# First scores as 16 packed 32x32 tiles, an ordered table of steps, v in strips of 32 partitions

## The chip, the cores and the metric

One core of a Trainium2 chip runs the whole program in one launch. The metric is the device time of one execution in microseconds (us), the median of several. The core's engines work side by side, each through its own list of instructions strictly in order: TensorE (PE; its weight loads, PEld, overlap its matmuls), VectorE (DVE), ScalarE (ACT), GpSimd (POOL), and SyncE (SP), which here issues the loads and stores. They wait for each other through semaphores.

## What is computed

```python
def attn(qq, kk, vv):                       # softmax attention, scale 1/8
    s = scale * qq @ kk.T;  a = exp(s - s.max(-1)); return (a / a.sum(-1)) @ vv
pp  = attn(p, k, v)                         # 8 batches x 8 heads: 32 packed rows over 576 tokens of 64
x   = attn(q, pp, pp)                       # 576 tokens over the 32 packed rows
logits = x @ phi                            # soft MoE: 8 experts x 4 slots, softmax over all 4608 tokens
slot_out = relu((softmax0(logits).T @ x) @ w1) @ w2
y   = softmax1(logits) @ slot_out
out = (mish(y @ w_in)) @ w_out              # 512 -> 2048 -> 512
```

All is float32; w_in and w_out lie as 64-bit words in memory and are converted on the chip.

## The kernel before

It goes through three phases: attention with the gathering of the slots, batch by batch; eight experts; the MLP. Only the attention's code and the order of the first loads are changed.

A **batch** (b) has its 8 heads in two groups of four (hq, and h4 within it). For each group, q and k arrive as one tile of 128 partitions (4 heads x 32 rows of 18 tokens). `tr_kq` transposes such a tile on VectorE in blocks of 32x32 (two transposes of 512 columns and one of 128). For k the destination of the large ones is interleaved by 4 elements; for q it is runs of 32. In v's tile partition 4r+a holds tokens that match this.

**First scores** (`s1`, p against k): p of four heads lies block-diagonally in a 128x128 weight, `pBD`, written by `bd_p`; k's transposed tile streams through, 4 matmuls of 288 columns for a group. `s1_act` takes the maximum over 576 columns on VectorE (`nmx`) and the exponential with its sum on ScalarE. `e1t` transposes the exponentials on TensorE (n = 0, 1: the groups; n = 2: the rest of 64 tokens) and ScalarE copies them out. `pv` multiplies them by v, `pv_c` scales, `pv_bd` transposes the packed rows and `pv_dg` writes them into a block-diagonal weight `ppBD` with four copies of 32 partitions.

**Second scores** (`s2`, q against the packed rows) come in two parts, z = 0 and 1: matmuls, `s2_mx` (maximum and difference, VectorE), `s2_exp` (ScalarE), `s2_norm` (sum and reciprocal, VectorE), `s2_mul` (GpSimd). `at` transposes them, `gmat` is the packed rows times phi, `lt` the logits. The steps `r_*` gather the slots with a running maximum: `r_mx`, `r_mr`, `r_row`, `r_d`, `r_de`, `r_dt`, `r_u`, `r_sel`, `r_si`.

What sets the order: the calls stand one after the other as written, and each engine's list follows from them. In the loop over b, second scores of batch b, `e1t` and `pv` of b+1, first scores of b+2 and the gathering of b-1 are interleaved. After the loop the last two batches run out, mixed with the conversion of the first eight w_in tiles (`cv_z`, `cv_u`, `cv_m`) and with idle matmuls as fillers (`warm1`). PSUM tiles of all small products share three buffers (`ps_t`), so each waits for the one three before it to be read out.

**Loads** are a list of jobs on SyncE's queue: for each batch k of b+2, v of b+1, q of b+1; then eight w_in tiles, then w1 and w2 of the experts with the rest of w_in between, then w_out. `pump` issues the next job when its buffer in a ring is free; a job waits there for everything ahead of it. `vr` (the last two tokens of each row of v) has two buffers, so vr of batch b waits for `pv` of batch b-2. The experts' tiles need the rings' places, and the first of them come free when expert 0 has run its first product (`hp`).

Of the kernel before, what the change touches and what calls it, by code (L numbers as in the profile page):

```python
# [9 lines left out]
F32 = mybir.dt.float32  # L10
# [9 lines left out]
def kernel(  # L20
# [22 lines left out]
    NB = 5  # L43
# [132 lines left out]
    for nm, b in (("k", 0), ("v", 0), ("q", 0), ("k", 1)):  # L176
        add_qkv(nm, b)
# [40 lines left out]
    e1_0 = win[2][:, 2 * HQ * D:2 * HQ * D + S]  # L218
    pT = win[0][:, 0:2 * B * HQ * J].rearrange("p (a c j) -> p a c j", c=2, j=J)
# [3 lines left out]
    def load_phi():  # L223
# [17 lines left out]
    pBD, ppBD = (  # L241
        [w.rearrange("p (b q c j) -> p b q c j", b=2, q=HQ, c=2)[:, i] for i in range(2)] for w in (win[1], win[3])
    )
    for t in pBD + ppBD:
        nc.gpsimd.memset(t, 0.0)
    warm = ps_s1.tile([128, 2, 512], F32, name="s1", tag="s1")
    for i in range(5):
        nc.tensor.matmul(warm[:, 0, 0:256], lhsT=ident, rhs=pBD[1][:, 0].rearrange("p c j -> p (c j)"), start=True, stop=True)
    load_phi()
    ids = const.tile([128, 32], F32, name="ids")  # L250
    idrep = const.tile([128, 128], F32, name="idrep")

    def consts2():
        nc.vector.reduce_sum(out=ids, in_=ident.rearrange("p (g m) -> p m g", g=4), axis=AX.X)
        nc.vector.tensor_copy(out=idrep.rearrange("p (g m) -> p g m", g=4), in_=ids[:, None, :].to_broadcast([128, 4, 32]))
# [22 lines left out]

    def cv_u(nm, i, name, dst, z, tv, fold):
# [17 lines left out]
    bgq = []  # L297

    def bg(n):

        for _ in range(n):
            if bgq:
                bgq.pop(0)()

    def bg_early():
        ts = [[] for _ in EARLY]
        z = [lambda t=t, x=x: t.extend(cv_z(*x)) for t, x in zip(ts, EARLY)]
        bgq.extend(z[0:2])
        for j, t in enumerate(ts):
            bgq.extend(lambda f=f, t=t: f(*t) for f in (cv_u, cv_m))  # L310
            bgq.extend(z[j + 2:j + 3])

# [9 lines left out]
    def tr_kq(nm, b, hq):  # L322
# [3 lines left out]
        main, rem = (slice(0, 512), slice(512, 576)) if nm == "k" else (slice(64, 576), slice(0, 64))  # L326
        st[b][nm + "T", hq] = T
        for dh in range(2):
            nc.vector.transpose(  # L329
                out=T[:, dh, main].rearrange(  # L330
                    "p (i r a) -> p a i r" if nm == "k" else "p (i a r) -> p a i r", i=4, a=4,
                ),
                in_=x[:, 0:16 * D].rearrange("p (a i dh dl) -> p dh a i dl", a=4, i=4, dh=2)[:, dh],
            )
        nc.vector.transpose(
            out=T[:, :, rem].rearrange("p dh (i r) -> p i dh r", i=2),
            in_=x[:, 16 * D:18 * D].rearrange("p (i dh dl) -> p i dh dl", i=2, dh=2),
        )
# [10 lines left out]
    def bd_p(b):  # L349
        if b < 2:  # L350
            return diag(pBD[b % 2], pT[:, b * HQ:(b + 1) * HQ], scale)
        for h4 in range(4):
            r = slice(32 * h4, 32 * h4 + 32)
            nc.gpsimd.tensor_scalar_mul(out=pBD[b % 2][r, :, :, r], in0=pT[r, b * HQ:(b + 1) * HQ], scalar1=scale)

    def s1(b, hq):
        d = st[b]
        kT = d.pop(("kT", hq))
        if hq == 0:
            d["sm"] = t1.tile([128, HQ], F32, name="sm1", tag="sm1")  # L360
        if (b, hq) == (0, 1):
            ps = ps_s2.tile([128, 2, 512], F32, name="s1", tag="s2_1")
        else:
# [1156 lines left out]
```

## Time and profile before

| what | value |
|---|---|
| median of 3 runs (lowest, highest) | 658.74 us (657.58, 659.43) |
| profiled execution | 660.98 us, of which the span 659.2 us |
| TensorE, VectorE, ScalarE, GpSimd busy in the span | 619.2 (94%), 502.6 (76%), 338.9 (51%), 57.3 us (9%) |
| chain that ended last, by engine | PE 73%, DVE 14%, DMA 5%, ACT 4% |
| moved by the queues | 89.61 MB, nearly all in the first 250 us |

The shares mix three phases with different limits, so they say little of the attention, which ends at about 164 us. Stretches are read one by one: in each, the engine whose busy time comes nearest to the stretch's length leads, and the share of the DMA queues says whether loads could go faster.

### The profile page before, as it was taken

Reading aid. Unit: us, or ns where it says so; the run is one execution under the profiler, and the core shown is the slowest. Engines: PE = TensorE matmul, PEld = TensorE weight load, DVE = VectorE, ACT = ScalarE, POOL = GpSimd, SP = SyncE. Lnnn points to the kernel's source line nnn. Section 1 sums busy time; section 2 is a strip of 40 time slices with the busy share of each in tenths; the row PEclk is TensorE's granted clock in tenths of the full one; section 3 lists DMA queues with packets and bytes.
Section 4 is the critical chain, followed back from the end, with each engine's and each line's share of the span. In section 5 each row is a group of like instructions: output and inputs, shape, how many; then the busy total and the mean of one; then the engine's idle time right before and its main releaser. Section 6 shows DMA issues by size and latency. Waiting matters only on the chain.

```text
span 659.2 us, 14426 instructions
## 1 busy us (share of the span) xinstructions
PE 619.2 (94%) x5878; PEld 533.4 (81%) x5878; DVE 502.6 (76%) x997; ACT 338.9 (51%) x681; POOL 57.3 (9%) x78
## 2 busy tenths in 40 slices
PE   7899999998969969999999999999999999999996
PEld 5677777776315538888888999999999999999996
DVE  5998888796571188988688987887788778877883
ACT  3344555645431367655364655555555555555551
POOL 5122222121040040000000000000000000000000
PEclk9899999997979989999999999999999999999998
DMA  8998946997799981011101100110011001100111
GB/s 285 325 295 315 310 156 239 402 397 290 243 397 403 393 354 33 0 33 33 32 1 33 33 16 18 33 33 17 18 33 33 21 14 33 33 25 9 33 33 33
DMA packets 42354, 89.61 MB, mean 136 GB/s; under 512 B 10928, under 2 KB 19248, under 8 KB 42288
## 3 DMA queue, kind: packets, MB, share of 16 engines
q1 hardware_dynamic: 41840, 88.36, 38.5%
q8 instruction: 46, 0.75, 0.5%
q10 hardware_dynamic: 192, 0.26, 0.2%
q14 instruction: 20, 0.16, 0.1%
q0 software_dynamic: 256, 0.07, 0.0%
HBM read 79.23 MB, written 9.44 MB: 135 GB/s over the span
## 4 chain that ended last, share of the span: by engine, by line
PE 73%; DVE 14%; DMA 5%; ACT 4%; issue 1%; SPq 1%; POOL 0%; DVEq 0%; ACTq 0%; POOLq 0%
PE o L1316 42%; PE so L1316 14%; PE h L1201 5%; DVE kT L329 4%; DMA r_w<-in_moe_w_dram 3%; PE hp L981 2%; PE so L1008 2%; DVE A L501 1%; DMA r_p<-in_p_dram 1%; DVE mx L500 1%; PE cp L1060 1%; PE s L481 1%; DVE nmx L377 1%; PE s L814 1%; ACT AT L539 1%
## 5 line engine op out<-in xcount | busy, mean ns | idle before, releaser
L1316 PE MATMUL o<-whi,gh 128*128 128x256 f32 (+1 forms) x444 | 117.5, 309 | 3.3 <-DVE osb L1357 2.2
L1316 PE MATMUL o<-wlo,gh 128*128 128x256 f32 (+1 forms) x444 | 116.5, 307 | 0.0
L1232 ACT CAST gh<-s 128x512 fp32r<-128x512 f32 x116 | 53.8, 511 | 109.4 <-PE o L1316 109.4
L1206 ACT ACTIVATE s<-h 128x512 f32<-128x512 f32 x144 | 83.7, 594 | 49.8 <-PE h L1201 49.7
L1316 PE MATMUL o<-whi,gl 128*128 128x256 f32 (+1 forms) x444 | 95.5, 305 | 0.0
L1316 PEld LDWEIGHTS o<-whi,gh 128*128 128x128 f32 x444 | 83.4, 190 | 8.1 <-ACT Sh L1233 2.4
L1316 PEld LDWEIGHTS o<-wlo,gh 128*128 128x128 f32 x444 | 84.2, 190 | 4.7
L1235 DVE TENSOR_TENSOR gl<-s,gh 128x512 fp32r<-128x512 f32 x116 | 59.5, 554 | 34.9 <-ACT gh L1232 34.9
L1236 DVE TENSOR_TENSOR Sl<-S,Sh 128x1024 fp32r<-128x1024 f32 x58 | 70.9, 1223 | 10.4 <-ACT Sh L1233 8.9
L1316 PEld LDWEIGHTS o<-whi,gl 128*128 128x128 f32 x444 | 71.5, 188 | 4.5
L1316 PE MATMUL o<-T,Sh 128*128 128x256 f32 x464 | 73.8, 281 | 0.0
L1316 PEld LDWEIGHTS o<-T,Sh 128*128 128x128 f32 x464 | 63.1, 188 | 0.0
L1233 ACT CAST Sh<-S 128x1024 fp32r<-128x1024 f32 x58 | 60.9, 1050 | 3.4 <-DVE S L1217 2.1
L1217 DVE TENSOR_TENSOR S<-s 128x256 f32<-128x256 f32 x116 | 48.8, 421 | 14.9 <-ACT s L1206 14.9
L1201 PE MATMUL h<-CS,MS 128*128 128x256 f32 x288 | 55.8, 284 | 0.0
L1316 PE MATMUL o<-T,Sl 128*128 128x256 f32 x232 | 46.9, 284 | 0.0
L1201 PEld LDWEIGHTS h<-CS,MS 128*128 128x128 f32 x288 | 44.0, 188 | 2.2 <-issue 1.0
L1357 DVE TENSOR_TENSOR osb<-osb,o 128x256 f32<-128x256 f32 x86 | 32.7, 417 | 8.2 <-PE o L1316 5.0
L1316 PE MATMUL so<-T,Sh 128*128 128x256 f32 (+1 forms) x232 | 38.6, 289 | 0.0
L367 PE MATMUL s<-kT,win 128*128 128x288 f32 x128 | 34.8, 415 | 2.8 <-ACT win L379 2.5
L1316 PEld LDWEIGHTS o<-T,Sl 128*128 128x128 f32 x232 | 35.9, 190 | 0.0
L481 PE MATMUL s<-win,qT 128*128 128x128 f32 x256 | 33.5, 286 | 1.8 <-ACT win L347 1.8
(254 smaller groups left out, 1132.1 us busy)
## 6 DMA issues: line engine op xcount, KB each, us to landing
r_w<-in_moe_w_dram SPq DMA_DIRECT2D x63, 512.0 KB, 10.5
r_k<-in_k_dram SPq DMA_DIRECT2D x16, 576.0 KB, 7.4
r_q<-in_q_dram SPq DMA_DIRECT2D x16, 576.0 KB, 4.8
r_v<-in_v_dram SPq DMA_DIRECT2D x64, 128.0 KB, 5.5
r_wi<-in_moe_w_in_dram SPq DMA_DIRECT2D x16, 512.0 KB, 9.1
r_wo<-in_moe_w_out_dram SPq DMA_DIRECT2D x16, 512.0 KB, 8.8
out_dram<-osb SPq DMA_DIRECT2D x64, 128.0 KB, 2.2
vr<-in_v_dram SPq DMA_DIRECT2D x16, 64.0 KB, 2.6
```

The costliest lines, as they stand in the source:

```text
L329: nc.vector.transpose(out=T[:, dh, main].rearrange("p (i r a) -> p a i r" if nm == "k" else "p (i a r) -> p a i r", i=4, a=4,), in_=x[:, 0 ...
L367: nc.tensor.matmul(ps[:, n, 0:288], lhsT=pBD[b % 2][:, hq, dh], rhs=kT[:, dh, 288 * n:288 * n + 288], start=(dh == 0), stop=(dh == 1),)
L481: nc.tensor.matmul(ps[:, k - lo], lhsT=d["qT", hq][:, dh, 64 + 128 * i:192 + 128 * i], rhs=ppBD[b % 2][:, hq, dh], start=(dh == 0), stop=( ...
L1201: nc.tensor.matmul(hp[:, 256 * f:256 * f + 256], lhsT=MS[:, 128 * ft:128 * ft + 128], rhs=CS[:, 256 * n:256 * n + 256], start=True, stop=True,
L1206: nc.scalar.activation(out=s, in_=hp.rearrange("p (f n) -> p f n", f=2), func=AF.Mish)
L1217: nc.vector.tensor_tensor(out=S[:, k], in0=x, in1=y, op=op)
L1232: nc.scalar.copy(out=gh[:, f, t], in_=s[:, f, t])
L1233: nc.scalar.copy(out=Sh, in_=S)
L1235: nc.vector.tensor_tensor(out=gl[:, f, t], in0=s[:, f, t], in1=gh[:, f, t].bitcast(F32), op=ALU.subtract)
L1236: nc.vector.tensor_tensor(out=Sl, in0=S, in1=Sh.bitcast(F32), op=ALU.subtract)
L1316: nc.tensor.matmul(o, lhsT=lhsT, rhs=rhs, start=first, stop=stop)
L1357: add = lambda o, x, y: nc.vector.tensor_tensor(out=o, in0=x, in1=y, op=ALU.add)
```

## The change

- **First scores in tiles.** `s1` does both groups of a batch at once: 32 matmuls of 32 rows by 32 columns, each row strip one head of four (h4), each column strip one of four combinations of group and half of the tokens (th). The weight is p transposed as it is, scaled in place; `pBD` and `bd_p` are gone. The results of the four h4 go to four PSUM banks, in the buffers of tags s1 and s2_1. Each head's tokens now lie in two halves on different partitions, so the maxima of the two halves meet through a matmul with a swapped negative identity (`s1_sw`) and a minimum (`s1_nm`); four exponentials of 288 columns follow; the sums meet through a selection matrix (`s1_sum`, 8 matmuls).
- **Transposes.** The k tile's transposes write runs of 32; those of q's 16x64 part are one instruction instead of two. `e1t` n = 2 becomes 8 ordinary matmuls of 32 columns against the identity, copied out in two pieces.
- **v.** A group of v comes in four DMAs, each to 32 partitions, 4 heads at once (runs of 1 KB as before), in the order of strips 0, 2, 1, 3. Before, it was one DMA per head to 128 partitions.
- **Queue.** k of batch 1 stands ahead of v and q of batch 0.
- **Order.** A table of named steps (`STEPS`) and three texts: HEAD, LOOP (50 steps and more, once each for b = 2, 3, 4) and TAIL. Copies out of PSUM are steps of their own (`e0c`, `a0c`, `dc`). In names, k0, k1, q0, q1 are transposes of the two groups, m, x, n, l with a or b the maximum, exponential, sum and product of the second scores' two parts, a0 to a2 `at`, bd and dg `pv_bd` and `pv_dg`. The last batch's second scores come in two parts instead of three; the buffers of transposed q and k are given to the weights after the last second scores; fillers drop from 21 matmuls to 6.

```diff
     def job_v(b, hq):
         def emit(t):
-            for h4 in range(4):
+            for a in (0, 2, 1, 3):
                 nc.sync.dma_start(
-                    out=t[:, 4 * h4 * D:4 * h4 * D + 4 * D],
-                    in_=v[b, 4 * hq + h4].rearrange("(r j) d -> r (j d)", j=18)[:, 0:16 * D].rearrange(
-                        "r (a x) -> r a x", a=4,
-                    ),
+                    out=t[32 * a:32 * a + 32, 0:16 * D].rearrange("r (h x) -> r h x", h=4),
+                    in_=v[b, 4 * hq:4 * hq + 4].rearrange("h (r j) d -> r h (j d)", j=18)[:, :, 4 * D * a:4 * D * a + 4 * D],
                 )
...
-    for nm, b in (("k", 0), ("v", 0), ("q", 0), ("k", 1)):
+    for nm, b in (("k", 0), ("k", 1), ("v", 0), ("q", 0)):
...
+        if nm == "k":
+            for th in range(2):
+                nc.vector.transpose(
+                    out=T[:, :, 288 * th:288 * th + 256].rearrange("p dh (i a r) -> p a i dh r", i=2, a=4),
+                    in_=x[:, 0:16 * D].rearrange("p (a t i dh dl) -> p t a i dh dl", a=4, t=2, i=2, dh=2)[:, th],
+                )
...
+    def s1(b):
...
+        for dh in range(2):
+            for hq in range(HQ):
+                for th in range(2):
+                    c = 64 * hq + 32 * th
+                    for h4 in range(4):
+                        r = slice(32 * h4, 32 * h4 + 32)
+                        nc.tensor.matmul(
+                            ps[h4 // 2][c:c + 32, h4 % 2, 0:288], lhsT=pT[r, b * HQ + hq, dh],
+                            rhs=kT[hq][r, dh, 288 * th:288 * th + 288], start=(dh == 0), stop=(dh == 1),
+                        )
...
+        for i, ps in enumerate(st[b]["s1"]):
+            nc.vector.reduce_max(out=mx[:, 2 * i:2 * i + 2], in_=ps[:, :, 0:288], axis=AX.X)
...
+        nc.tensor.matmul(sw, lhsT=minus_sw, rhs=st[b]["mx1"], start=True, stop=True)
...
+        nc.vector.scalar_tensor_tensor(out=nm, in0=d.pop("mx1"), scalar=-1.0, in1=d.pop("sw"), op0=ALU.mult, op1=ALU.min)
...
+        for i in range(4):
+            nc.scalar.activation(
+                out=d["e1"][i], in_=ps[i // 2][:, i % 2, 0:288], func=AF.Exp,
+                bias=nm[:, i:i + 1], scale=1.0, accum_out=d["sm"][:, i:i + 1],
+            )
...
+                nc.tensor.matmul(
+                    rp[32 * h4:32 * h4 + 32, hq:hq + 1], lhsT=sel[:, hq], rhs=d["sm"][:, h4:h4 + 1], start=True, stop=True,
+                )
...
         for h4 in range(4):
...
+            for th in range(2):
                 nc.tensor.matmul(
...
+                    tp[32 * th:32 * th + 32, h4], lhsT=d["e1"][h4][:, 256:288], rhs=ident, start=True, stop=True,
                 )
...
+    LOOP = """
+        s2a rmx mr k1 e0 e1 row e0c d s2b e1c dc ma k0 de dt xa mb e2 dtc na e2c xb us nb sum sumc s1 usc da la pv sel
+        mx1 pvc lb a0 a2 selc a1 a0c q1 sw bd a2c a1c dg nm si lt ltc q0 exp gm gmc sic
+    """
```

The order as built shows three places. In its rows stand the line, the operation, the tile written and those read, the shape and the number in a row; numbers at a tile's name tell buffers apart, `win` tiles hold p, block-diagonal weights and exponentials.

TensorE's list before, middle of the loop: e1's transposes, the first scores of the first group (`s_1236`), gathering, `pv` and the first scores of the second group.

```order
L398 MATMUL e_ps<-ident,e_1156 128x128 x4
L403 MATMUL e1r_ps<-ident,win_95 64x128
L403 MATMUL e1r_ps<-ident,e_1156 64x128
L367 MATMUL s_1236<-kT,win_94 128x288 x4
L608 MATMUL dp<-ident,dT 128x128
L610 MATMUL dp<-ident,dT 64x32 x2
L419 MATMUL pv<-r_v_0_305,e1T 32x64 x16
L419 MATMUL pv<-vr,e1T 32x64 x4
L419 MATMUL pv<-r_v_1_330,e1T 32x64 x16
L419 MATMUL pv<-vr,e1T 32x64 x4
L367 MATMUL s_1313<-kT,win_94 128x288 x4
```

The same place in the changed kernel: the last two pairs of the first scores' 32 matmuls (14 pairs like them stand ahead), then `pv`, the transposes and the swap of the maxima.

```order
L360 MATMUL s_1157<-kT,win_93 32x288 x2
L360 MATMUL s_1158<-kT,win_93 32x288 x2
L453 MATMUL pv<-r_v_0_172,win_94 32x64 x16
L453 MATMUL pv<-vr,win_95 32x64 x4
L453 MATMUL pv<-r_v_1_177,win_94 32x64 x16
L453 MATMUL pv<-vr,win_95 32x64 x4
L692 MATMUL uq<-ids,up 128x32 x2
L571 MATMUL at<-ident,A 128x128 x4
L575 MATMUL atr<-ident,A 128x128
L571 MATMUL at<-ident,A 128x128 x4
L375 MATMUL sw<-mx_1244,minus_sw 128x4
```

Both groups' first scores now stand together ahead of `pv`, and the transposes `at` of the second scores right behind it.

ScalarE's list before, from the first group's exponential (`win_95`) to the second's (`e_1924`).

```order
L379 ACTIVATE win_95,sm_1747<-s_1748,nmx 128x576
L508 ACTIVATE A<-A 128x640
L428 ACTIVATE pp<-pv,r_1670 128x64 x2
L601 ACTIVATE al<-nM 128x1
L347 ACTIVATE win_96<-ppT 32x4x32 x4
L641 COPY up<-us 128x256
L456 COPY G<-gp 128x64
L656 COPY U<-uq 128x64
L539 COPY AT<-at 128x512 x2
L543 COPY AT<-atr 128x2x64
L379 ACTIVATE e_1924,sm_1747<-s_1825,nmx 128x576
```

ScalarE's list in the changed kernel, from the scaling of `pv` to the copy of G at the end of an iteration.

```order
L462 ACTIVATE pp<-pv,r_1748 128x64 x2
L699 COPY U<-uq 128x64
L581 COPY AT<-at 128x512
L583 COPY AT<-atr 128x2x64
L581 COPY AT<-at 128x512
L340 ACTIVATE win_96<-ppT 32x4x32 x4
L601 COPY LT<-lp 128x128
L602 COPY LT<-lp 32x64
L392 ACTIVATE win_95,sm_1905<-s_1751,nm 128x288 x2
L392 ACTIVATE e_1906,sm_1905<-s_1752,nm 128x288 x2
L490 COPY G<-gp 128x64
```

All four exponentials stand together behind the diagonal copies (`win_96`) and the logits' copies.

SyncE's list at the start of the program, before.

```order
L113 DMA r_k_0_99<-in_k_dram 128x1152
L113 DMA r_k_1_101<-in_k_dram 128x1152
L121 DMA r_v_0_103<-in_v_dram 128x1x256 x4
L121 DMA r_v_1_108<-in_v_dram 128x1x256 x4
L131 DMA vr<-in_v_dram 32x8x64 x2
L113 DMA r_q_0_116<-in_q_dram 128x1152
L113 DMA r_q_1_118<-in_q_dram 128x1152
L113 DMA r_k_0_120<-in_k_dram 128x1152
L113 DMA r_k_1_122<-in_k_dram 128x1152
```

SyncE's list at the start of the changed kernel.

```order
L113 DMA r_k_0_99<-in_k_dram 128x1152
L113 DMA r_k_1_101<-in_k_dram 128x1152
L113 DMA r_k_0_103<-in_k_dram 128x1152
L113 DMA r_k_1_105<-in_k_dram 128x1152
L121 DMA r_v_0_107<-in_v_dram 32x4x256 x4
L121 DMA r_v_1_112<-in_v_dram 32x4x256 x4
L129 DMA vr<-in_v_dram 32x8x64 x2
L113 DMA r_q_0_120<-in_q_dram 128x1152
L113 DMA r_q_1_122<-in_q_dram 128x1152
```

The second batch's keys moved past the first batch's ten v loads and two q loads, and each v load now has 32 partitions by 4 heads.

## Rows read from the trace of the kernel before

**Rows 1.** Busy time by stretch; entries in brackets, then TensorE's granted clock, DMA share, GB/s.

```profile
core 0: us, PE busy (x) PEld busy (x) DVE busy (x) ACT busy (x) POOL busy (x), PEclk, DMA share, GB/s
5.80:58.30 52.50, 45.97 (x621) 35.40 (x621) 45.37 (x91) 23.57 (x68) 14.13 (x22) 0.97 0.96 322
58.30:104.60 46.30, 44.07 (x652) 35.30 (x650) 40.65 (x87) 23.23 (x70) 9.78 (x13) 1.00 0.64 212
75.90:93.30 17.40, 16.37 (x253) 13.03 (x253) 14.92 (x33) 9.17 (x28) 4.36 (x6) 1.00 0.80 273
104.60:160.50 55.90, 51.17 (x759) 40.10 (x759) 45.30 (x107) 31.07 (x93) 12.06 (x14) 0.97 1.01 388
160.50:168.50 8.00, 7.13 (x56) 3.90 (x58) 3.78 (x10) 1.38 (x4) 0.00 (x0) 0.55 0.03 11
168.50:228.00 59.50, 50.73 (x653) 21.65 (x645) 23.67 (x55) 19.26 (x33) 8.02 (x9) 0.94 1.01 379
...
127.80:163.90 36.10, 32.56 (x431) 25.71 (x429) 27.94 (x69) 18.79 (x54) 6.44 (x7) 0.91 0.93 358
235.00:659.20 424.20, 410.09 (x3074) 389.96 (x3074) 340.13 (x643) 233.19 (x400) 8.11 (x5) 0.99 0.12 34
```

**Rows 2.** Chain of work that ended last, in order of time: start, us, what.

```profile
58.61 2.00 DVE kT L329 x2
...
75.99 1.99 DVE kT L329 x2
...
163.94 0.72 PE sit_ps L943 x8
...
175.12 1.72 PE hp L981 x16
```

**Rows 3.** SyncE's queue in order of time: start, us, DMA, what it loads.

```profile
102.22 1.34 SPq L131 DMA_DIRECT2D vr<-in_v_dram  x2
...
104.64 4.67 SPq L159 DMA_DIRECT2D r_wi<-in_moe_w_in_dram  x8
...
151.16 17.44 SPq L138 DMA_DIRECT2D r_w<-in_moe_w_dram  x4
```

**Rows 4.** Waits of SyncE's queue: total us, times, longest.

```profile
SPq L131 <- PE pv L419: 12.7, 3, 10.0
```

**Rows 5.** Timeline inside one batch of the loop: start, us, engine, instructions.

```profile
79.63 0.38 PE L586 MATMUL mp<-ident,nrep 1*128 1x1 f32 x2
...
80.65 2.11 PE L367 MATMUL s<-kT,win 128*128 128x288 f32 x8
...
81.11 0.46 ACT L593 ACTIVATE dT<-LT,nM 128x192 f32<-128x192 f32 x1
...
84.28 0.74 ACT L379 ACTIVATE win<-s,nmx 128x576 f32<-128x576 f32 x1 [0.32 <-DVE nmx L377]
...
85.17 2.21 PE L367 MATMUL s<-kT,win 128*128 128x288 f32 x8 [0.41 <-ACT win L379]
...
87.32 1.26 ACT L347 ACTIVATE win<-ppT 32x128 f32<-32x128 f32 x4 [0.99 <-DVE ppT L434]
...
88.12 0.34 PEld L448 LDWEIGHTS gp<-phi_sb,ppT 32*32 32x32 f32 x32
```

**Rows 6.** Groups by shape, 0 to 220 us: busy us, mean ns, idle before.

```profile
L329 DVE STREAM_TRANSPOSE kT<-r_k 128x512 f32<-128x512 f32 x32 | 32.5, 1093 | 2.3 <-DMA r_k<-in_k_dram 2.3
...
L329 DVE STREAM_TRANSPOSE qT<-r_q 128x512 f32<-128x512 f32 x32 | 20.3, 673 | 0.1
```

**Rows 7.** Timeline at the start: first key transpose, with its idle time and releaser.

```profile
5.82 2.01 DVE L329 STREAM_TRANSPOSE kT<-r_k 128x512 f32<-128x512 f32 x2 [2.29 <-DMA r_k<-in_k_dram]
```

**Rows 8.** Busy time by stretch as in rows 1: first v load, two stores.

```profile
6.20:9.20 3.00, 2.79 (x9) 1.43 (x9) 3.00 (x5) 0.00 (x0) 2.89 (x5) 1.00 1.09 334
293.50:294.00 0.50, 0.50 (x6) 0.46 (x5) 0.50 (x1) 0.31 (x1) 0.00 (x0) 1.00 1.01 230
655.50:656.00 0.50, 0.00 (x0) 0.00 (x0) 0.00 (x0) 0.00 (x0) 0.00 (x0) 0.80 0.96 275
```

More of the change, by code (lines that the diff above doesn't have):

```diff
@@ L240 @@
     make_identity(nc, ident)
[L241 to L244, printed above, removed]
+    ppBD = [win[3].rearrange("p (b q c j) -> p b q c j", b=2, q=HQ, c=2)[:, i] for i in range(2)]
+    for t in ppBD:
         nc.gpsimd.memset(t, 0.0)
@@ new lines, in s1 @@
+    def s1(b):
+        d = st[b]
+        kT = [d.pop(("kT", hq)) for hq in range(HQ)]
+        ps = [
+            ps_s1.tile([128, 2, 512], F32, name="s1", tag="s1"),
+            ps_s2.tile([128, 2, 512], F32, name="s1", tag="s2_1"),
+        ]
+        for dh in range(2):
+            for hq in range(HQ):
[7 more added lines that the diff above has]
+                        )
+        d["s1"] = ps
@@ new lines, in s1_exp @@
+    def s1_exp(b):
+        d = st[b]
+        nm = d.pop("nm")
+        d["sm"] = t1.tile([128, 4], F32, name="sm1", tag="sm1")
+        e1 = (e1_0, t1.tile([128, S], F32, name="e1", tag="e1", bufs=1))
+        d["e1"] = [e1[i // 2][:, 288 * (i % 2):288 * (i % 2) + 288] for i in range(4)]
+        ps = d.pop("s1")
+        for i in range(4):
[3 more added lines that the diff above has]
+            )
@@ L367, in s1, with s1_sum @@
+    def s1_sum(b):
+        d = st[b]
+        rp = ps_t.tile([128, HQ], F32, name="r1p", tag="t")
+        for hq in range(HQ):
+            for h4 in range(4):
                 nc.tensor.matmul(
-                    ps[:, n, 0:288], lhsT=pBD[b % 2][:, hq, dh], rhs=kT[:, dh, 288 * n:288 * n + 288],
-                    start=(dh == 0), stop=(dh == 1),
-                )
-        d["s1", hq] = ps
-    def s1_act(b, hq):
+                    rp[32 * h4:32 * h4 + 32, hq:hq + 1], lhsT=sel[:, hq], rhs=d["sm"][:, h4:h4 + 1], start=True, stop=True,
+                )
+        d["rp"] = rp
@@ L394, in e1t @@
[L394 to L404 removed]
+        tp = ps_t.tile([128, 4, 128], F32, name="e1_ps", tag="t")
@@ new lines, in e1t, with e1t_c @@
+        if n < 2:
+            for h4 in range(4):
+                nc.tensor.transpose(tp[:, h4], d["e1"][h4][:, 128 * n:128 * n + 128], ident)
+            d["tp", n] = tp
+            return
+        for h4 in range(4):
+            for th in range(2):
+                nc.tensor.matmul(
+                    tp[32 * th:32 * th + 32, h4], lhsT=d["e1"][h4][:, 256:288], rhs=ident, start=True, stop=True,
+                )
+        d["tp", n] = tp
+    def e1t_c(b, n):
+        tp = st[b].pop(("tp", n))
+        if n < 2:
+            nc.scalar.copy(out=e1T[:, n], in_=tp)
+            return
+        v = tp.rearrange("p h (q t j) -> p t h q j", q=HQ, t=2)
+        for th in range(2):
+            r = slice(32 * th, 32 * th + 32)
+            nc.scalar.copy(out=e1Tr[r], in_=v[r, th])
@@ new lines @@
+    """
+    seq = [x.split(".") for x in HEAD.split()]
+    for b in range(2, B - 3):
+        seq += [(name, b + STEPS[name][0]) for name in LOOP.split()]
+    seq += [x.split(".") for x in TAIL.split()]
+    last_q = max(i for i, (name, b) in enumerate(seq) if name in ("s2a", "s2b"))
+    for i, (name, b) in enumerate(seq):
+        b = int(b)
+        if (name, b) == ("bd", 0):
+            nc.vector.transpose(
+                out=pT[:, 2 * HQ:].rearrange("p a c j -> p (a c j)"), in_=take("p")[:, 0:(B - 2) * HQ * D],
+            )
+            done("p")
+            scale_p(2, B - 2, nc.gpsimd)
+            consts2()
+        if name == "warm":
+            warm1(b)
+        else:
+            STEPS[name][1](b)
+        if i == last_q:
+            slots[2][0] = slots[3][0] = ring_x
+            pump()
```

425 lines of the change are left out of this document (107 added, 318 removed).

## The prediction

> **What bounds the kernel now.** I read the stretches first, then the chain of work that ended last, then SyncE's queue. The profiled execution took 660.98 us (span 659.2), 2.2 us above the median of three runs, 658.74; the sum below is a difference and is taken off both.
>
> The span has three parts. Up to 163.9 us runs the attention, the experts follow, and from about 235 us the MLP, which keeps TensorE busy for 410 of 424 us with almost no loads [rows 1]; the change does not touch it. In the attention one batch takes 17.4 us: the same pair of key transposes starts at 58.61 and at 75.99 [rows 2]. In one such batch TensorE is busy for 16.37 us and VectorE for 14.92 [rows 1]: TensorE leads, VectorE is close behind, and an edit has to relieve both.
>
> There is a second bound: the loads. From 104.6 us, where SyncE gets past vr of the last batch, the weights stream without a pause (share 1.01) to 160.5; then nothing moves for 8 us (share 0.03) until the first expert has read its w1 tiles; then the stream is full again to 228 [rows 1, 3]. So the experts run at the speed of the loads, and they end earlier by as much as **the later of two things** comes earlier: the first expert's release of its tiles (168.5) and the filling of the tiles (160.5). A faster attention has 8 us to win there before the loads set the end. What held the stream back before 104.6 is SyncE waiting for pv two batches earlier, since vr has two buffers (12.7 us in 3 waits) [rows 4]: in 58.3 to 104.6 the queues are busy 0.64 of the time, so 16.7 us are idle [rows 1].
>
> **The change, part by part.**
>
> *TensorE, first scores.* A batch now spends two groups of 8 trace entries on them, 2.11 and 2.21 us [rows 5]; 0.1 of each overlaps the next group, so 4.1 us. They multiply a block-diagonal p, three quarters zeros. After, there are 32 matmuls, 64 entries, each 32 rows by 32 columns by 288. One entry streams for 2.11/8 = 0.26 us [rows 5]. If all 16 tiles run at once, that is 4 rounds, 1.05 us. Loading 64 small weights hides in it: 32 loads of 32x32 take 0.34 us in gp [rows 5]. If only four run at once it is 4.2 us. Four column strips at once are shown: hp's 16 entries of 512 columns take 1.72 us, 0.108 each, where one alone would be 0.26 x 512/288 = 0.46 [rows 2]. Row strips at once under one column strip are shown by no row. I take 1.2, near the full packing, because the strips that are shown reach their full factor.
>
> The Trainium skill, "TensorE: Matmul & The Clock Gate", part 3, reports 10.6 times for 16 tiles of 32x32, not 16. By that ratio, an estimate, the first scores take 64 x 0.26/10.6 = 1.6 us and each batch 0.4 us more than I take; no run here shows it yet.
>
> *TensorE, what comes in.* The rest of e1's transpose becomes 8 ordinary matmuls on two column strips: 16 entries of 128 columns, 0.46/4 = 0.115 each, two at once, 0.9 us, where two entries took 0.23: +0.7. The swap of maxima (sw) is one matmul of a 128-column weight, as mp is: 0.4 [rows 5]. The sums (sum) are 16 tiny entries, 0.2 at the rate of gp's weight loads. TensorE's batch: 16.37 - 4.1 + 1.2 + 0.7 + 0.4 + 0.2 = **14.8 us**.
>
> *VectorE.* The key transposes write runs of 32 as the query ones do: 1093 ns falls to about 673 by the query row [rows 6]. A pair of keys takes 2.0 us [rows 2], so I count 0.35 for each, not 0.42: four a batch, -1.4. Merged query transposes save 0.1, nm costs 0.2; the two maxima read as many columns as before. 14.92 - 1.3 = 13.6.
>
> *ScalarE and GpSimd.* Four exponentials of 288 columns replace two of 576. From 0.74 us for 576 and 0.46 for 192 [rows 5] one of 288 is 0.53: 2.1 for 1.5. With one more copy ScalarE goes from 9.17 to about 10.2, not the bound. But in the table the exponentials stand behind the four diagonal copies (1.26 us, [rows 5]) at the end of an iteration, and the next one's e0 waits for them; second scores s2a stand between on TensorE and cover nearly all of it. The scaling of p on GpSimd leaves the loop; it was hidden.
>
> *One batch of the loop.* Before, 17.4 = 16.37 busy + 1.0 waiting. I keep the 1.0, now the wait for exponentials and diagonal copies, and get 15.8, rounded down to 15.6 because the ends of the short new groups overlap their neighbours; bounds 14.7 (no wait) and 16.6. Four iterations (three of LOOP and the first of TAIL, which repeats its order for batch 5) save 4 x 1.8 = **7.2** (3.2 to 10.8).
>
> *The head.* The first key transpose starts at 5.82, when its load lands [rows 7]. From there to 58.3 VectorE has 45.4 us of work and 7.1 idle [rows 1]. Eight key tiles, 16 x 0.35 to 0.42, leave: -6; merges -0.5, nm +0.8: 39.7. Queueing 1.18 MB of k(1) ahead of v(0) and q(0) puts these 1.18/0.334 = 3.5 us later (334 GB/s in v's first load, [rows 8]); VectorE has k(1)'s tiles to do in that time (about 3 us), so I add 0.5 of idle: 5.8 + 39.7 + 7.6 = 53.1, **-5** (-3 to -7).
>
> *The end of the attention.* From 127.8 to 163.9 VectorE works 27.9 of 36.1 us [rows 1]; the same work remains, spread in another order, with the last two batches interleaved. I take **-1.5**. It could be -4, if VectorE is kept as full as in the loop, and +2, if the fillers, cut from 21 matmuls to 6, let TensorE's clock fall earlier than now (0.55 of 2.4 GHz in 160.5 to 168.5, mostly its lower level, [rows 1]).
>
> Sum at the attention's end: 7.2 + 5 + 1.5 = **13.7 us**; the first expert's release moves from 168.5 to 154.8.
>
> *The loads.* Does the stream follow? With pv of batch 5 about 7.6 us earlier (head 5, two iterations of 1.8, less 1 because pv stands later in its iteration), the weights could start at 97.0 and fill the tiles at 97.0 + 55.9 = 152.9, before 154.8. But v is now loaded by eight DMAs to 32 partitions. v's 1.05 MB of a batch go at 334 GB/s now, 3.1 us [rows 8]. Loads to 32 partitions of this kind aren't in the trace; the nearest rows are stores from 32 partitions, 230 and 275 GB/s at full queue share [rows 8]: 4.6 or 3.8 us, +0.7 to +1.5 a batch. Without idle the q, k, v stream would end at 104.6 - 16.7 = 87.9; eight batches of +0.7 to +1.5 make it 93.5 to 99.9; the tiles are full at 152.9 to 155.8. So the stream just keeps up; I take 13 us of the 13.7.
>
> **Forecast: 13 us off, 646 us (648 as profiled).** Own range: gains of 5 to 20, 638.5 to 654.
>
> **The rivals.**
>
> *v's loads fall to half rate or less and the weights come late (the other side).* If a load to 32 partitions gets half of what one to 128 gets, 167 GB/s, it takes 6.3 us, +3.2 a batch: q, k, v end at 113.5, the tiles are full at 169, no gain: 659. The turning point is 1.05 MB/(3.1 + 3.1) = 170 GB/s. At 150, +3.9 a batch, the tiles are full at 175 and the kernel takes about 665. Against it stand the stores at 230 and 275. The SBUF page of the Trainium skill ("SBUF — State Buffer", Door 1) states it as a rule: 32 partitions reach half the ports, 189 GB/s at 1 MiB against 328 for all 128; and under "Can I just issue two DMAs to hit both halves?" two such loads at once gain only 6%. By 189 GB/s, an estimate, v takes 5.6 us, the tiles are full at 164, and 654 is left. That is in my range; the stores at 275 speak for more. Chance 0.14: 0.07 slower, 0.04 no change, 0.03 faster.
>
> *The 16 tiles run four at a time.* First scores 4.2 us, a batch 14.7 + 3.0 + 1.0 = 18.7 or 1.3 above today, 5.2 in four; the head keeps some 3 of its 5, the end its 1.5: about 660. A microsecond more costs 4 in the loop and some 0.7 in the head, so the 13.7 are gone at 1.2 + 2.9 = 4.1 us for a batch's first scores. For it: no row shows row strips together. Against: gp's 32x32 tiles go through about as fast as their weights load [rows 5]. Chance 0.05, 0.02 of it slower.
>
> *The change gives more than I see:* period 14.7, head -7, tail -4 make 21.8 at the attention's end; but the tiles are full at the earliest at about 149, so the loads keep 19.5: 639. Chance 0.06, in the range.
>
> **How the numbers follow.** Forecast 0.75; v's loads 0.14; four tiles 0.05; more 0.06. Two microseconds, 0.3%, is about what a measurement of this kernel tells from no change. Faster: 0.75 + 0.06 + 0.03 = 0.84; same 0.04 + 0.03 = 0.07; slower 0.07 + 0.02 = 0.09. The range from 638 to 656 takes in the larger gain and the mild form of the slow v.
>
> **What would show it.** Starts of key pairs 15.6 us apart in the middle. First scores of a batch in 1.0 to 1.6 us; near 4 the second rival holds. Key transposes near 0.67 us each. The attention's last transpose (sit_ps) ending near 151. First weights issued near 97 to 100, and the pause ahead of the first expert gone from the loads, 8 us to 0 to 2. A pause that stays, with the first expert waiting for nothing, would mean the gain is the attention's alone; weights that start after 105 mean slow v. I am wrong if the 50 steps, each engine taking them strictly in turn, wait for each other for more than 2 us a batch, or if the clock falls inside the loop.

## The result: 1.1% slower, where 2% faster was forecast

The changed kernel takes 667.59 us (median of four, 664.43 to 669.92) against 659.09 of the kernel before (657.58 to 659.81): ratio 1.0109, 95% interval 1.0072 to 1.0147. The forecast was 646. The profiled execution took 669.2 us (span 667.4).

The end tells where to look. From the last transpose of the attention (sit_ps) to the end the kernel before needs 659.2 - 163.94 = 495.3 us [rows 2], the changed one 667.4 - 169.37 = 498.0. So the attention, forecast to end 13.7 us earlier (150.2), ends 5.4 later: 19 us are missing there. Traces, here and below, show one execution of each kernel; the changed kernel's is 1.6 us slower than its median.

What the change does to single operations came as forecast. Views of one line or tile of the kernel after (line, engine, operation, count, min/median/max ns), against 1093 ns in [rows 6]:

```profile
L320 DVE STREAM_TRANSPOSE kT<-r_k x32: 668/673/712, 5.4 to 117.3; 128x512 f32<-128x512 f32 x32
L326 DVE STREAM_TRANSPOSE qT<-r_q x16: 1201/1234/1245, 18.2 to 143.4; 128x1024 f32<-128x1024 f32 x16
```

One iteration of the loop did, too, where nothing disturbs it: the products with v start at 107.30 and at 122.48, 15.2 us apart, where 15.6 was forecast and 17.4 was. But the one ahead of it takes 22.1. Busy time by stretch, kernel after, columns as in [rows 1]: two iterations that went badly, the middle of the second, the clean one, the end of the attention, the pause ahead of the first expert:

```profile
67.84:107.29 39.45, 33.67 (x667) 27.07 (x662) 28.21 (x66) 20.34 (x66) 4.80 (x5) 0.91 0.86 242
84.00:96.90 12.90, 8.99 (x227) 7.18 (x194) 6.42 (x17) 4.47 (x16) 2.31 (x2) 0.74 0.90 269
107.30:122.48 15.18, 15.05 (x339) 12.16 (x332) 13.28 (x29) 10.10 (x33) 2.15 (x2) 1.00 0.80 288
158.40:169.40 11.00, 9.39 (x104) 5.98 (x96) 5.29 (x15) 4.09 (x15) 0.56 (x2) 0.50 0.80 291
170.00:175.00 5.00, 4.61 (x26) 1.17 (x28) 2.16 (x5) 0.72 (x1) 0.00 (x0) 0.50 0.00 0
```

In that middle (84.00 to 96.90) nobody is busy: TensorE 9.0 of 12.9 us, VectorE 6.4, and the clock is at 0.74. Its timeline (start, us, engine, line, instructions, idle before) shows why:

```profile
83.62 1.60 PE L360 MATMUL s<-kT,win 32*32 32x288 f32 x64
85.15 0.65 PE L453 MATMUL pv<-r_v,win 128*32 128x64 f32 x32
85.74 0.32 PE L453 MATMUL pv<-vr,win 64*32 64x64 f32 x8
85.98 0.54 PE L453 MATMUL pv<-r_v,win 128*32 128x64 f32 x23
90.43 0.48 PE L453 MATMUL pv<-r_v,win 128*32 128x64 f32 x9 [3.91 <-issue]
90.83 0.44 PE L453 MATMUL pv<-vr,win 64*32 64x64 f32 x8
91.20 1.06 PE L692 MATMUL uq<-ids,up 128*128 128x32 f32 x4
```

The products with v stop after 23 of 32 entries on one tile of v and go on 3.9 us later with the other nine. v of that batch was queued at 57 to 67 us; it is not what is waited for. "issue" says that no other engine and no load is. Behind it four uq entries take 1.06 us instead of 0.63: half clock, from 90.1 to 96.9. Such pauses stand in the waits of TensorE of the kernel after (engine, what, released by: us in all, times, longest); the same list of the kernel before, up to 175 us, has no wait for "issue" at a matmul:

```profile
PE pv L453 <- issue: 6.1, 4, 3.9
PE gp L482 <- issue: 3.1, 2, 1.8
PE lp L591 <- issue: 1.1, 1, 1.1
```

**What they have in common** is seen by numbering TensorE's entries in the trace (weight loads, matmuls, semaphore entries) in order of time, from 0. Six pauses up to 150 us, each with the number of the first matmul behind it:

```
ends at us   length   entry number      ahead of it a 16 KB packet of the
                                        instruction queue began, us earlier
55.3         1.07     1729 =  6*256+193    2.61
68.8         0.42     2241 =  8*256+193    2.60
75.1         1.32     2497 =  9*256+193    2.44
90.4         3.91     3009 = 11*256+193    2.70
124.6        1.52     4290 = 16*256+194    2.38
131.3        1.77     4546 = 17*256+194    2.40
```

They stand whole multiples of 256 entries apart (give or take one, where a weight load comes first), whatever the operation, and each ends 2.4 to 2.7 us after a packet of 16 KB on one instruction queue. That queue carries 51 such packets for TensorE's 13107 entries, and 46 for 11840 in the kernel before: one for 256 entries. So TensorE waits for its program. The blocks behind which it waits had run in 2.9 to 5.6 us, but a short block is not enough: entries 705 to 961 ran in 3.9 us without a pause, since the next packet began 1.3 us behind the block's start, and ahead of the pause at 3009 it began 4.1 us behind. Between one batch's products with v and the next lie 675 entries, where the kernel before has 508: with weight loads the first scores are 128 entries instead of 32, the sums 32 new ones, e1's last transpose 28 more. I call such a pause a halt; together they are 10.0 us. The kernel before has none in its attention, but one of 0.77 us among the experts, at 216.5: entry 5313 = 20*256+193, 2.4 us behind its packet, after a block that ran in 5.5 us. So halts were not new, only frequent.

The Trainium skill ("Runtime: NRT & Kernel Launch", "Instruction fetch mechanics") says the same of the size, blocks of 16 KB with 256 instructions, and calls the cost of crossing "mostly hidden". Here six crossings show, with 10.0 us.

The second suspect is the load of v. In the packet records v's 8192 packets of 1 KB take 72 ns (median) in the strips of 32 partitions, where they took 46 before: 16 engines at 1 KB in 72 ns are 228 GB/s, and 8192 x 26 ns / 16 make 13.3 us more in eight batches, 1.66 a batch. SyncE's queue, kernel after, against [rows 3, 4]:

```profile
109.08 0.81 SPq L129 DMA_DIRECT2D vr<-in_v_dram  x2
...
110.95 6.23 SPq L157 DMA_DIRECT2D r_wi<-in_moe_w_in_dram  x8
```

```profile
SPq L129 <- PE pv L453: 6.7, 1, 6.7
```

The weights start at 110.95 instead of the 97 forecast. But vr waited 6.7 us for the products with v; the loads were ahead of the attention, not behind.

### The profile page after: what moved, and what is told of

It is laid out like the page before. It is cut to its first block, busy times and chain, and to the rows that moved or that the text cites. A ratio compares the mean times of both kernels' runs of the same rounds, so it can differ in the third digit from the quotient of the medians.

```text
span 667.4 us, 15674 instructions
## 1 busy us (share of the span) xinstructions
PE 621.2 (93%) x6488; PEld 532.1 (80%) x6488; DVE 493.2 (74%) x986; ACT 344.4 (52%) x712; POOL 45.6 (7%) x54
## 4 chain that ended last, share of the span: by engine, by line
PE 65%; DMA 3%; DVE 2%; issue 0%; ACT 0%; SPq 0%; DVEq 0%; ACTq 0%
PE o L1201 42%; PE so L1201 14%; PE h L1086 5%; DMA r_w<-in_moe_w_dram 3%; PE cp L945 1%; PE so L893 1%; DVE osb L1242 1%; PE mp L1034 1%; PE hp L866 1%; PE mp L1042 0%; DVE w L290 0%; DVE gl L1111 0%; PE so L1042 0%; DVE r_wo L287 0%; DVE h1T L886 0%
## 5 line engine op out<-in xcount | busy, mean ns | idle before, releaser
L515 PE MATMUL s<-win,qT 128*128 128x128 f32 x256 | 36.3, 303 | 0.6 <-DVE win L338 0.5
L515 PEld LDWEIGHTS s<-win,qT 128*128 128x128 f32 x256 | 33.9, 214 | 1.5 <-ACT win L340 0.6
## 6 DMA issues: line engine op xcount, KB each, us to landing
r_w<-in_moe_w_dram SPq DMA_DIRECT2D x63, 512.0 KB, 10.4
```

The source lines that it names most:

```text
L515: nc.tensor.matmul(ps[:, k - lo], lhsT=d["qT", hq][:, dh, 128 * i:128 * i + 128], rhs=ppBD[b % 2][:, hq, dh], start=(dh == 0), stop=(dh == 1),
```

## The experiments

Theory A: v's slow strips are the loss. Theory B: the halts are, for a program that is too dense. Ratios are to the kernel before, in runs on the same chip.

**1. v by head over 128 partitions.**

```
-            for a in (0, 2, 1, 3):  strip a to t[32a:32a+32]
+            for h4 in range(4):     head h4 to t[:, 256*h4:256*h4+256],  in_.rearrange("r (a x) -> a r x", a=4)
```

> The changed kernel with one thing put back: v again comes one head at a time over all 128 partitions (four loads of 128 KB a block, as before the change), only with partition 32a+r for the chunk that the 16-tile scores want. In the changed kernel a 1 KB packet of v took 72 ns (median) where it took 46 ns before, which for the 8192 packets is 13.3 us of the 16 DMA engines. Theory A (the strips of 32 partitions are the whole loss: data of the batches comes late): packets back at 46 ns, q, k and v through by about 93, weights from 98 to 104, no halt of TensorE in the loop, total 645 to 650 us. Theory B (TensorE halts because its own program comes too late: six halts of 0.4 to 3.9 us, 10.0 us in all, each a whole number of 256 instructions behind the one before, each ending 2.4 to 2.6 us after a 16 KB packet of the instruction queue began, with half clock behind four of them): the packets are at 46 ns but halts stay at the same instructions wherever 256 of them pass in under about 6 us; total 652 to 664 us.

Measured: 704.62 us, 1.0652 (1.0599 to 1.0705). Neither theory. The packets took 49 ns, but while v is in flight:

```profile
50.00:55.00 5.00, 4.71 (x64) 4.40 (x65) 3.94 (x9) 3.72 (x16) 0.00 (x0) 0.50 0.28 91
```

A share of 0.28 and 91 GB/s are about those of four of 16 engines. The source pattern now begins with a dimension of four. The run says nothing on strips; it is a lesson of its own. The Trainium skill ("DMA: Bandwidth & Descriptors", "Why a DMA increments its semaphore by 16 and not by 1") has the rule: the number of engines is the largest up to 16 that divides both patterns' slowest dimensions, here four. The trace agrees.

**2. Strips alone, in the kernel before.**

```
-   "p (i r a) -> p a i r" if nm == "k" else "p (i a r) -> p a i r"
+   "p (i a r) -> p a i r"
+   v by the changed kernel's strips
```

> The kernel before with v's strips alone: v comes in strips of 32 partitions as in the changed kernel, and the key transposes write their columns in plain order so that keys and v's rows still match (this takes them from 1093 to about 680 ns, 1.6 us less VectorE work a batch). First scores, order of the steps and queue are those of before. Theory A (strips alone cost the time): v's packets at about 72 ns, 13 us more of DMA work, batches late, total 662 to 672 us. Theory B (the strips' 13 us fit into the 16.7 us in which DMA idled between 58 and 105 us, and the loss comes from the denser TensorE program): no halts of TensorE of over 0.5 us for want of its program, total 654 to 661 us.

Measured: 656.70 us, 0.9943 (0.9918 to 0.9967). The packets take 71 ns, and it is faster than the kernel before, with no halt in the attention; an iteration takes 17.05 us. A is refuted as a cause by itself: strips and cheaper key transposes together come out ahead. What the strips cost alone is not separated from what the transposes give. This is the fastest kernel of the study with the whole computation.

**3. The grid moved by 128 instructions.**

```
+    for i in range(32):
+        nc.tensor.matmul(warm[0:32, 1, 0:1], lhsT=ident[:, 0:32], rhs=ident[:, 0:1], ...)
```

> The changed kernel with 32 tiny multiplies (one column, 64 passes, 128 TensorE instructions, about 1.3 us in the idle start) added behind the five warming ones; everything else is as in the changed kernel. Theory B (program pages of 256 instructions): counted in the records the halts of TensorE keep their remainder modulo 256 (193 of 256), so in the program they fall 128 instructions earlier than in the changed kernel, beside other operations than the products with v and the G products of before; total 660 to 672 us, by where the grid falls. Theory A (the products with v wait for v): the halts stay at the same operations, and the remainder moves by 128; total 667 to 669 us.

Measured: 670.02 us, 1.0131 (1.0077 to 1.0184). Waits of TensorE in 20 to 150 us:

```profile
PE uq L694 <- issue: 4.6, 2, 3.4
PE pv L455 <- issue: 2.7, 1, 2.7
PE lp L593 <- issue: 0.9, 1, 0.9
```

The halts up to 150 us are now at lp, at the products with v and twice at uq, at entries 1218, 1730, 2498 and 4545 (8.2 us in all), each 193 or 194 beyond a multiple of 256, so 128 instructions earlier in the program: three of these numbers had a halt in the changed kernel, at lp and twice at gp. In what follows them two iterations of 15.2 us stand in a row (products with v at 94.35, 109.53, 124.71). B holds: it is the count of instructions, not the operation, that decides where TensorE stops.

**4. v as before, in the new order.**

```
-            for a in (0, 2, 1, 3):  strip a
+            for h4 in range(4):     as before the change ("r (a x) -> r a x")
-    k columns "p dh (i a r) -> p a i dh r"
+    k columns "p dh (i r a) -> p a i dh r"
```

> The changed kernel with v loaded exactly as before (one head at a time, row 4r+a, 1 KB packets at 46 ns and all 16 DMA engines at work, which the load by head onto rows 32a+r had not: its share of 0.27 to 0.28 was that of four engines) and with key columns written in that order, which costs the key transposes their old stride (0.42 us more for each of four, 1.7 us of VectorE a batch, in a loop where VectorE has room). The order of the steps, the queue and the 16-tile scores stay. Theory A (slow strips are the loss): 13 us of DMA work less, 646 to 652 us. Theory B (halts for the TensorE program): 675 instructions a batch as in the changed kernel, halts at a whole number of 256 apart stay, 5 to 10 us of them in all with half clock behind, 658 to 670 us.

Measured: 664.43 us, 1.0068 (1.0034 to 1.0102). Packets at 46 ns; of the halts two are left, 1.07 and 2.31 at entries 2241 and 4289. The total is in B's range, the halts (3.4 us) are fewer than its 5 to 10, and the loop comes back. Busy time by stretch for the two iterations that took 39.5 us above, kernel with v as before:

```profile
69.57:102.10 32.53, 30.67 (x667) 24.59 (x662) 30.35 (x63) 20.56 (x66) 4.66 (x5) 1.00 0.68 217
```

The clock is full throughout, and one halt of 1.07 us is left of three in this place. The reading that fits is B with a part of A in it: from the entry where a block begins to the next packet of the instruction queue there passed 3.1 us on the mean up to 110 us in the changed kernel, 2.1 here. The block ahead of entry 3009 shows what that does: 2.9 us long and its packet 4.1 us behind its start in the changed kernel, halt 3.91; 3.1 us long and its packet 0.9 behind here, no halt. So the strips do harm, not by late data but by delaying the program's packets, as far as pairs of traces tell: with v in strips and as before the mean is 3.2 and 2.4 in the kernel before, 2.6 and 2.2 with the old queue of experiment 8, 3.1 and 2.1 with the tail fillers of experiment 9, but 2.4 and 2.4 in experiment 6. Why a packet starts late was not settled. 6.6 us of halts are gone and 0.4% of the time, 2.7 us, came back (the two intervals overlap); the head is 3.8 later (products with v of the third batch at 52.7 instead of 48.8), at half clock from 8.8 to 22.5 and 25.9 to 32.7.

**5. The kernel before, made dense.**

```
+        for _ in range(40):
+            nc.tensor.matmul(ps[0:32, 0, 0:1], lhsT=ident[:, 0:32], rhs=ident[:, 0:1], ...)
```

> The kernel before with 40 multiplies of one column (80 passes, 160 TensorE instructions of about 20 ns a pass, 1.6 us a batch) put ahead of each batch's products with v, in the place where the changed kernel has its first scores: 668 instructions a batch instead of 508 (675 in the changed kernel). v, keys, queue and order of the steps are those of before. By arithmetic alone: TensorE's 16.4 of 17.4 us a batch become 18.0, so 662 to 670 us, without halts. Theory B: halts of 0.4 to 4 us appear in the loop, ending 2.4 to 2.6 us after a packet of the instruction queue begins and whole multiples of 256 instructions apart. Theory A: no such halts.

Measured: 687.18 us, 1.039 (1.030 to 1.048). One halt only in the attention, 1.82 us, at entry 1473 = 5*256+193, ended 2.4 us after its packet. The rest of the 28 us was not foreseen: the 80 passes take 2.5 us instead of 1.6, and behind them the clock falls to its lower level for 3.4 us in four of the batches (from 98.9, 119.4, 139.9 and 153.6) and for 6.8 in a fifth, the one with the halt. For B it is weak evidence; 668 entries in 20.5 us are hardly denser than 508 in 17.4.

```profile
96.09 2.66 PE L411 MATMUL pv<-ident 128*32 128x1 f32 x79
...
99.73 1.08 PE L421 MATMUL pv<-r_v,e1T 128*32 128x64 f32 x32
```

**6. Fewer instructions, same result.**

```
-  gp[r, hq] <- ppT[r, hq, dh] * phi_sb[r, hq, dh]        (16 matmuls of 32x32)
+  gp[:, hq] <- ppBD[b % 2][:, hq, dh] * phi_sb[:, hq, dh] (4 matmuls of 128x128)
-  rp <- sel[:, hq] * sm[:, h4]                           (8 matmuls)
+  W = sel * sm on GpSimd;  rp[:, hq] <- W[hq] * one_c     (2 matmuls)
```

> The changed kernel with 72 TensorE instructions a batch fewer (603 instead of 675) and the same result: the G products go over 128 rows with the block-diagonal queries that the second scores use anyway (8 passes in place of 32), and the row sums of the first softmax are collected by 2 products over 128 columns (4 passes in place of 16) from a table that GpSimd multiplies ahead. v's strips stay. Theory B: the pages of 256 last longer, halts together 10.0 us fall to 3 to 7 us, 658 to 665 us. Theory A: the strips still cost their 13 us, 666 to 670 us.

> Both of the foregoing at once: v as before with keys' columns in that order, and 603 TensorE instructions a batch. Theory A: as v as before alone, 646 to 652 us. Theory B: the DMA queues are lighter and the pages longer, so 650 to 660 us; if halts stay at over 5 us in all, 660 to 668.

Measured: 676.13 us, 1.021 (1.014 to 1.028), and with v as before 669.50, 1.013 (1.006 to 1.020). Both expectations failed, and the edit is to blame: G over 128 columns takes 1.08 us instead of 0.45 and waits for the diagonal copies, so a clean iteration takes 16.2 us. The halts did fall, from 10.0 to 5.8 us, and to one of 2.3 with v as before. Total time doesn't tell the theories apart here.

**7. Half of the first scores.**

```
-        for dh in range(2):
+        for dh in range(1):
```

> The changed kernel with the second half of the depth left out of the first scores (32 of the 64 entries a batch; the scores are those of the first 32 of 64 numbers of each head, all else runs as before on them): 611 TensorE instructions a batch instead of 675, and 0.5 to 0.8 us less TensorE time. Strips and queue as in the changed kernel. Theory B (halts for program pages): the densest 256 instructions last longer, halts in the loop fall from 10.0 to 2 to 6 us, 655 to 663 us. Theory A (strips hold the loop): 664 to 668 us, the gain no more than the 0.8 us a batch that TensorE is spared, if that.

Measured: 660.35 us, 0.9971 (0.9937 to 1.0005); halts 4.1 us. 7.2 us below the changed kernel and both figures as B says, though work is missing. The trace tells how much that is worth in the loop: with no halt between them, two iterations take 29.86 us (products with v at 66.99 and 96.85), 14.93 each, where the changed kernel's clean one takes 15.2. So in the loop the missing work is worth some 0.3 us an iteration, and most of the gain must come from elsewhere; the halts are 5.9 us fewer.

**8. The queue of before.**

```
-    (("k", 0), ("k", 1), ("v", 0), ("q", 0))
+    (("k", 0), ("v", 0), ("q", 0), ("k", 1))
```

> The changed kernel with the queue of before: k, v and q of the first batch, then k of the second. Steps, strips and scores as in the changed kernel. In the changed kernel q's first tile is waited for until 18.17 us (VectorE idle for 3.35), and the products with v of the first batch begin at 19.5, where they began at 14.3 before. If the queue is what held the head back (theory H1): that wait falls below 1.5 us, the first products with v begin 2 to 3 us earlier and all behind them too, 663 to 666 us. If the head is held by its own chain of small steps on a TensorE at half clock (theory H2): VectorE now waits for keys of the second batch instead, the products with v of the third batch begin at 47 to 51 us as before, total 666 to 671 us.

> The changed kernel with v's loads (and key columns) and the queue of before: only the 16-tile scores, the new order of the steps and the merged transposes of queries are left of the change. With v as before alone it took 664.4, its products with v of the third batch at 53.1 (48.8 in the changed kernel), since at half clock from 9.3 to 23.0 and 26.4 to 33.2. H1: 3 us earlier behind the first q, 659 to 662. H2: 663 to 667.

Measured: 667.72 us, 1.0089 (1.0055 to 1.0124), and with v as before 663.71, 1.0056 (1.0027 to 1.0085): both as the changed kernel and as experiment 4, so the queue's order is worth nothing measurable. q's first transpose starts at 21.4 instead of 18.2, since the steps ask for the second batch's keys first, and VectorE now waits 3.09 us for those, where it waited 3.35 for q:

```profile
18.32 1.30 DVE L320 STREAM_TRANSPOSE kT<-r_k 128x512 f32<-128x512 f32 x2 [3.09 <-DMA r_k<-in_k_dram]
```

H1 falls. H2's total holds; the third batch's products with v, at 53.7, are later than it had them.

**9. Fillers in the head, in the tail.**

```
+  HEAD: wt.6 ahead of sw.0, wt.5 ahead of e0.0, wt.8 ahead of gm.0
+  TAIL: wt.7 ahead of d.6, wt.2 ahead of d.7 and of dt.7      (wt.n: n matmuls ident x ident)
```

> The changed kernel with 19 filling multiplies (128x128 by 128 columns, about 0.23 us each) at three places of the head where TensorE idles (behind the first scores of the first batch, ahead of its first transpose, ahead of its G products); the rest is the changed kernel. There TensorE ran at half clock from 11.6 to 18.4 and 25.3 to 28.7, and the products with v of the third batch began at 48.8, where the forecast had about 44.6. If half clock holds the head (H2): they begin at 45 to 47 us, the attention ends 2 to 4 us earlier, total 663 to 667. If the head is held by loads and VectorE (q's first tile at 18.2): they begin at 48 to 50, total 667 to 670. The grid of 256 instructions moves by 76, so single halts in the loop move too, and their sum may change by some us either way.

> The changed kernel with 11 of the same fillers in the last 15 us of the attention, 7 of them where TensorE waits 1.57 us just ahead of its fall to half clock (158.4 to 175.5). The grid of instructions ahead of that place is that of the changed kernel. If the cut of the fillers costs the tail its clock, as the prediction feared: half clock shrinks to below 10 us there, from the last products with v to the last transpose of the attention 24 to 27 us instead of 28.6, total 663 to 666. If the tail's chain of small steps decides, and the clock does not come back or does not matter: 28 to 30 us, total 667 to 670.

Head: 665.43 us, 1.006 (1.0025 to 1.0095). Half clock ahead of 21.8 us is gone and the halts, at other places, come to 7.4 us; yet the third products with v start at 51.0, later than without fillers, and VectorE now waits 4.86 us for q. So the half clock of 11.6 to 18.4 does not hold the head. Half clock from 21.8 to 28.6 stayed, and this run does not speak on it. Tail: 663.73 us, 1.0041 (1.0010 to 1.0073). From the last products with v to sit_ps it takes 26.1 us instead of 28.6. Busy time by stretch, kernel with tail fillers, its last 11 us of attention:

```profile
152.80:163.80 11.00, 9.18 (x129) 6.44 (x127) 7.72 (x21) 6.01 (x21) 0.55 (x2) 0.97 1.04 400
```

The clock is 0.97 where the last 11 us of the changed kernel had 0.50 (158.40:169.40 above). Fillers in the tail keep its clock, and cutting them is the likely cost; the kernel before, with its 21, still had 10.2 us at half clock from 157.5 on.

**10. The causes together.** v as before and tail fillers; then also half of the scores.

> The changed kernel with v (and key columns) loaded as before and with 11 fillers in the attention's tail: two single changes together. Against the kernel before, the changed one stood at 1.0109, v as before alone at 1.0068 and the fillers alone at 1.0041. If the causes add: 1.0109 - 0.0041 - 0.0068 = 1.000, 658 to 662 us. If both took back the same time (the half clock that one execution happens to have): no better than the better of the two, 663 to 666 us.

> As the foregoing, and the second half of the depth left out of the first scores (607 TensorE instructions a batch, 0.8 us less TensorE work in each of 8 batches). Left out alone it gave 0.9971 against the kernel before, 7.2 us below the changed kernel. If the causes add: 0.9971 - 0.0041 - 0.0068 = 0.986, 649 to 653 us, halts in the loop below 2 us in all: then halts, strips and fillers together are most of the miss, with 5 us or so of the 0.8 us a batch left to the work that is missing. If it stays at 656 to 660, something else (the head, VectorE with its strided key columns) holds the attention once the halts are gone.

Measured: 660.83 us, 1.0023 (1.0002 to 1.0044): the two add, within the noise, and this interval is clear of the changed kernel's; halts of 4.9 us are left. And 655.56, 0.9931 (0.9901 to 0.9961), some 5 us above the sum, with halts of 3.1 us where less than 2 was expected; the attention ends at 156.6. Its products with v stand at 65.4 for the fourth batch (forecast 61.8) and at 96.9 for the sixth (92.8): the two iterations between are near the forecast, the head is not. What holds the head is left open.

## Why the prediction was wrong

The prediction puts the products with v of the fourth batch at 65.8 - 5 + 1 = 61.8 us (they were at 65.84) and those of the sixth at 100.4 - 7.6 = 92.8, the attention's end at 150.2. Measured: 67.8, 107.3, 169.4. So the miss of 19 us falls into three pieces. The first is explained by what the experiments show, the second is not, the third in the main.

- **The loop, 8.4 us** (39.5 for two iterations instead of 31.0). The step that failed is "one batch of the loop", 16.37 - 4.1 + 1.2 + 0.7 + 0.4 + 0.2 = 14.8. It counts TensorE's time and not its instructions, of which a batch now has 675 instead of 508. In this piece stand three halts (0.42, 1.32, 3.91) and 6.8 us at half clock, worth 3.4 at most: 9.1. That halts are the mechanism is shown by experiments 3 and 4: they go by the count of entries, and where two of these three are gone the two iterations take 32.5 us. The sum for a batch without halts, 15.6, came out at 15.2, partly by luck: TensorE is busy for 15.05 us instead of 14.8, and the 1.0 of waiting that the prediction keeps is 0.1. "The clock falls inside the loop" stands among the things that would make the prediction wrong, without a cause.
- **The head, 6.0 us.** The step is "I add 0.5 of idle" for q behind k(1): VectorE stood idle for 3.35 us ahead of q's first transpose, which starts at 18.17. One halt (1.07) and 3.4 us of half clock behind it are in this piece too. Putting the queue back did not help: with either queue VectorE waits more than 3 us for a load in this place, for q or for the second batch's keys, both of which the steps ask for ahead of the first products with v. What else holds the head was not settled.

```profile
18.17 1.25 DVE L326 STREAM_TRANSPOSE qT<-r_q 128x1024 f32<-128x1024 f32 x1 [3.35 <-DMA r_q<-in_q_dram]
```

- **The end, 4.7 us.** The step is "I take -1.5", which came out at +3.2, beyond the bound of +2 that named the cut fillers. Two halts (1.52, 1.77) lie here. And the bound's mechanism came true: 17.1 us at half clock (158.4 to 175.5) against 10.2 in the kernel before; with fillers (experiment 9) the stretch from the last products with v on is 2.5 us shorter. The first expert's products, still at half clock, take 6.10 us for their first 32 entries where 4.93 were enough before, and the pause ahead of it stayed (0 GB/s from 170 to 175).

**The first scores** take 1.60 us in a clean batch, where I took 1.2: 64 x 0.26 / 1.60 is a packing of 10.4. The Trainium skill's 10.6 ("TensorE: Matmul & The Clock Gate", part 3), set aside in the prediction, was nearer than the 14 that 1.2 us stands for.

**v's loads.** 228 GB/s is just under the row I took as the lower bound (230), so 1.66 us a batch instead of 0.7 to 1.5. The turning point of the first rival, 170, was not reached, and the weights started late because vr waited for the products with v, not because v was slow. The 665 that it gives for 150 GB/s is near the measured time by chance. What the step missed, by the reading of experiment 4, is a second customer of the DMA queues: the program's packets. The 189 GB/s of the Trainium skill ("SBUF — State Buffer", Door 1) was further off than the nearer of the stores' rows.

**The rivals** both priced slow data or slow tiles. The side they ended on came from neither. Of the two signs of being wrong at the end of the prediction, the clock fell inside the loop, but behind halts. Steps that wait for each other were not it: TensorE waited for its own program.

## What to carry to other kernels

Where an edit cuts big operations into small ones, count the instructions of the engine beside their time: here a block of 256 that ran in 2.9 to 5.6 us could make TensorE stop for its own program when the block's packet came late, and behind three of six stops the clock fell to its lower level. A pause that no engine and no load explains is dated by its number: if the entries between such pauses are multiples of 256, it is the program. Fillers that seem to do nothing can hold the clock of a chain of small steps (0.97 instead of 0.50 here); cutting them has a price.

## What the hardware showed that was not expected

- A halt ends 2.2 to 2.8 us after a 16 KB packet of the instruction queue begins, in some 50 halts in the attention of 14 kernels, at entry 193 or 194 beyond a multiple of 256. Experiment 1 has three of them (5.9 us); in one, 104.8 to 107.3, the share of the DMA engines is 0.27: not all of them need be at work.
- A load whose source pattern begins with a dimension of four moves 91 GB/s at a share of 0.28, that of about four DMA engines, though it writes all 128 partitions.
- v's packets of 1 KB take 46 ns to 128 partitions and 72 ns in strips of 32.
- Multiplies of one column keep TensorE busy in the records (20.23 of 20.50 us in a batch of experiment 5), and the clock still falls to its lower level behind them.
